# Attention's PSUM banks as two tiles of three and two single ones, with one exponential per three heads

## The chip, the cores and the metric

The kernel runs on one core of a Trainium2 chip, in fp32. The metric is the device time of one execution in microseconds (us). Engines are called as the profile calls them: PE (TensorE, matmuls; PEld are its weight loads), DVE (VectorE), ACT (ScalarE), POOL (GpSimd), SP (SyncE, which issues DMAs here).

## What is computed

One token matrix `x` of 2048 rows and 448 columns goes through an attention with 16 query heads and one shared key and value head (width 28), and through a token- and channel-mixing MLP. A gate mixes the two results:

```
g = sigmoid((x * gate_w).sum(-1))
q = (x @ wq) as 16 heads of 28;  k = x @ wk;  v = x @ wv
p = softmax(q k^T * 28**-0.5);   a = (p v, heads side by side) @ wo
b = x1 + gelu(layernorm(x1) @ w3) @ w4     where x1 = x + shifted gelu(layernorm(x) @ w1) @ w2
out = g * a + (1 - g) * b
```

The change lies in the attention, which fills the second part of the program, from about 400 us on. The MLP before it is left as it was.

## The kernel before

Scores are held with keys on the partitions. A **unit** `u` is one block of 512 queries with one group of four heads; there are 16 units. A unit runs over 16 key tiles `kt` of 128 keys, in 8 **stretches** `v` of two key tiles each. The loop at L1004 counts stretches through all units with `k` (0 to 126; the last stretch is written out behind the loop). All engines' orders are those in which the code is written: the kernel has a manual schedule, so each engine runs its instructions in the order of the Python calls.

In a stretch the following happens, in this order of the calls:

- `scores(u, kt)` (L937 to L943), for the first and then the second key tile. Four heads are computed side by side, each on 32 rows of PE, into four PSUM banks of 512 columns. Each product is split in three passes (`i` = 0, 1, 2 at L939), and the four heads of one pass come one after the other. So all four banks of a key tile are complete with its last pass.
- `exps` (L959). Heads 0, 1 and 2 go through an exponential on ACT from PSUM to SBUF, one instruction per head (L969), as softmax without division. Head 3 is copied by DVE to a tile `pd` (L966). The order in which the banks are read is `READ = (0, 3, 1, 2)`.
- `late_exps` (L974): one exponential on ACT, in place in SBUF, over head 3 of both key tiles (128x1024).
- The **job**: four matmuls of the output product of an earlier unit (`wo_half`, L865, with the matmuls at L843), 32 rows of tokens each, into one bank. DVE adds the result to the output tile (L837). In stretches 2 to 11 the job is a rest of the MLP (`w4_half`, L879). Stretch 0 has three larger ones instead (`w4_job`, L869), stretch 1 has none, and the last unit has two jobs in its last four stretches.
- `values` (L986): probabilities times values for the stretch before this one (`k - 1`), in two halves of 256 query columns. Each half is 16 matmuls into one bank (L979), for four heads side by side, and DVE adds the half to the tile `o` of the unit (L983; a copy at L994 in a unit's first stretch). DVE adds the first half when it is done, and the second in the next stretch's beginning.

The eight banks are in a queue `banks`. `take()` pops the oldest. A bank goes to the end of the queue when its reader has been issued. So a job takes the bank of the first key tile's first head (its exponential is the first to be issued), the first half of the values that of head 3, and the second half that of head 1. A wait is set from who used the bank last: the tiles are tracked one by one.

```
bs = [take() for j in range(4)]                      # L938
for j in READ: ... banks.append(bs[j])               # L961, L970
ps = take(); wo_part(...); evict(...); banks.append(ps)   # job
pv = take(); value(...) x2; add_value(...)           # a half of the values
```

Of the kernel before, what the change touches and what calls it, by code (L numbers as in the profile page):

```python
# [9 lines left out]
F32 = mybir.dt.float32  # L10
F32R = mybir.dt.float32r
AF = mybir.ActivationFunctionType
# [4 lines left out]
P = 128  # L17
S = 2048
D = 448
# [11 lines left out]
SHIFTS = (-1, 1, -2, 2)  # L31
PB = 18
PD = 3
# [9 lines left out]
def gated_mix_kernel(  # L43
# [15 lines left out]
    dram = ctx.enter_context(tc.tile_pool(name="dram", bufs=1, space=bass.MemoryType.DRAM))  # L59
    psA = ctx.enter_context(tc.tile_pool(name="psA", bufs=1, space=PSUM))  # L60
    ctx.enter_context(tc.manual_schedule(
# [136 lines left out]
    def max_tile(name):  # L198
        return psA.tile([P, 512], F32, tag="mx", bufs=1, name=name)
# [566 lines left out]
    ctx2.close()  # L766


    with tc.tile_pool(name="s3", bufs=1, reuse_waits="tile") as s3, \
# [3 lines left out]

        banks = [mm_tile("bank_0"), mm_tile("bank_1"), misc_tile("bank_2"), max_tile("bank_7")]
        banks += [ps3.tile([P, 512], F32, name=f"bank_{i}") for i in range(3, 7)]
# [70 lines left out]
        def wo_end(u, t, ps, evict=by_one, queue=nc.sync, cols=slice(0, D)):  # L846
            b, g = divmod(u, NG)
            n = 4 * b + t
            before = x1[:, n, cols] if g == 0 else ot_of[n][:, cols]
            evict(n, ps, before, cols)  # L850
            banks.append(ps)
# [5 lines left out]
        def wo_job(u, t, cols=slice(0, D), evict=by_one, queue=nc.sync):  # L857
            b, g = divmod(u, NG)
            ps = take()
# [3 lines left out]
            return wo_end(u, t, ps, evict, queue, cols)  # L863

        def wo_half(u, i):  # L865
            t, h = divmod(i, 2)
            wo_job(u, t, slice(224 * h, 224 * h + 224))

        def w4_job(t):  # L869
            n = NT - 4 + t  # L870
            tok = slice(t * P, (t + 1) * P)
            gh, gl = last_g
            ps = bank(f"job_{n}")[:, 0:D]
            nc.tensor.matmul(ps, gh[:, tok], w4h[-1][:, 1, :], start=True, stop=False)
            nc.tensor.matmul(ps, gh[:, tok], w4l[-1][:, 1, :], start=False, stop=False)
            nc.tensor.matmul(ps, gl[:, tok], w4h[-1][:, 1, :], start=False, stop=True)
            nc.vector.tensor_add(x1[:, n, :], x1[:, n, :], ps)

        def w4_half(k, i):  # L879
            t, h = divmod(i, 2)  # L880
            n = NT - 4 + t
            cols = slice(224 * h, 224 * h + 224)
            ps = take()
# [5 lines left out]
            banks.append(ps)  # L889

# [46 lines left out]
        def scores(u, kt):  # L937
            bs = [take() for j in range(4)]  # L938
            for i in range(3):  # L939
                for j in range(4):  # L940
                    for _, _, w, a in score(u, bs[j], j, slice(kt * P, (kt + 1) * P), i=i):
                        nc.tensor.matmul(bs[j], w, a, start=(i == 0), stop=(i == 2), tile_position=(32 * j, 0))  # L942
            return bs  # L943

        p_free = [s3.tile([P, 512], F32, name=f"p_{i}") for i in range(PB)]
        pd_free = [s3.tile([P, 2, 512], F32, name=f"pd_{i}") for i in range(PD)]
# [11 lines left out]

        def exps(u, kt, bs):  # L959
            ps = p_of[u, kt] = {}  # L960
            for j in READ:  # L961
                if j == DRAIN:
                    if kt % 2 == 0:
                        pd_of[u, kt // 2] = turn_of(pd_free)
                    ps[j] = pd_of[u, kt // 2][:, kt % 2, :]
                    nc.vector.tensor_copy(ps[j], bs[j])  # L966
                else:
                    ps[j] = turn_of(p_free)
                    behind[kt % 2] = nc.scalar.activation(ps[j], bs[j], AF.Exp, scale=SCALE)  # L969
                banks.append(bs[j])  # L970

# [10 lines left out]
        def add_value(u, q, pv):  # L982
            nc.vector.tensor_add(o_of[u][:, q], o_of[u][:, q], pv[:, q])  # L983
            banks.append(pv)

        def values(u, v):  # L986
            if v == 0:
                o_of[u] = s3.tile([P, 512], F32, tag="o", bufs=2, name=f"o_{u}")
            for q in HALVES:
                pv = take()  # L990
                for kt in (2 * v, 2 * v + 1):
                    value(u, kt, q, pv, kt % 2 == 0, kt % 2 == 1)
                if v == 0:
                    nc.vector.tensor_copy(o_of[u][:, q], pv[:, q])  # L994
                    banks.append(pv)
                else:
                    add_value(u, q, pv)

        HALVES = (slice(0, 256), slice(256, 512))

        READ = (0, 3, 1, 2)
        DRAIN = 3

        for k in range(NU * NV - 1):  # L1004
            u, v = divmod(k, NV)
            if k == 3:
                q_begin(1)
                q_fetch(2)
            if v == 6 and u + 2 < NU:
                q_begin(u + 2)  # L1010
                q_fetch(u + 3)
            for kt in (2 * v, 2 * v + 1):
                exps(u, kt, scores(u, kt))
            late_exps(u, v)
            if k == 0:
                for t in range(3):
                    w4_job(t)
            if k in (2, 3):
                w4_half(1, k + 4)
            if 4 <= k < 12:  # L1020
                w4_half(0, k - 4)
            if k == 11:
                weigh_x1(NT - 4, NT)
            if v >= 4 and u:
                wo_half(u - 1, v - 4)
            if v < 4 and u > 1:
                wo_half(u - 2, v + 4)
# [34 lines left out]

        blocks = [slice(4 * t, 4 * t + 4) for t in range(4)]
        b14, b15 = [scores(u, kt) for kt in (NT - 2, NT - 1)]
        p14 = p_of[u, NT - 2] = {j: turn_of(p_free) for j in range(DRAIN)}
        p14[DRAIN] = turn_of(pd_free)[:, 0, :]
# [3 lines left out]
        for q in HALVES:  # L1070
            for p, ps in [(p14[1], b14[1]), (p14[2], b14[2]), (p14[DRAIN], p14[DRAIN])] + [(p15[j], b15[j]) for j in READ]:
                nc.scalar.activation(p[:, q], ps[:, q], AF.Exp, scale=SCALE)
# [9 lines left out]
        banks.extend((b14[1], b14[2]))  # L1082
        add_value(u, q0, pvs[0])
        value(u, NT - 3, q1, pvs[1], False, False)
        value(u, NT - 2, q1, pvs[1], False, False)
# [9 lines left out]
        banks.extend(b15)  # L1095
        add_value(u, q1, pvs[1])
        tail_back(blocks[1])
        store0 = wo_job(u, 0, evict=by_two, queue=None)
# [4 lines left out]
        for n in blocks[2:4]:  # L1103
            tail_back(n)
        wo_end(u, 1, joint[1])
        nc.sync.dma_start(*store0)
        joint[3] = take()
# [9 lines left out]
        nc.scalar.activation(redo, tw, AF.Copy, scale=-1.0, bias=float(P))  # L1117
        wo_end(u, 3, joint[3], by_one, nc.scalar)
        again = nc.values_load(redo, min_val=0, max_val=P,
                               skip_runtime_bounds_check_because="it is P less a sum of P zeros and ones")  # L1120
# [60 lines left out]
```

## Time and profile before

| what | us |
|---|---|
| median of 3 runs (lowest, highest) | 911.42 (911.41, 911.49) |
| span of the profiled execution, first to last instruction | 909.8 |
| PE, ACT, DVE busy in the span | 904.0, 634.5, 543.7 |
| first stretch begins (scores of the first key tile) | 400.2 |
| the loop's last stretch ends | 895.4 |

The time of a run is 1.6 us longer than the span of the profiled execution; the trace has no other time for that execution than its span. A matmul's end in the profile is modelled, and four matmuls of a group run side by side. So "busy" for PE says little, and the starts of groups say more: they are given in rows of the timeline, with start and duration in us, engine, line, operation, `out<-in`, the shape, the count `x`, and in square brackets the idle time before with what ended it.

### The profile page before, as it was taken

To read this page: it belongs to the slowest core of one execution; us is meant where nothing else is said; L and a number is where in the kernel's file an instruction comes from. 1 tells how busy PE (TensorE), PEld (TensorE's weight loads), DVE (VectorE), ACT (ScalarE), POOL (GpSimd) and SP (SyncE) were. 2 spreads that over 40 slices of the span, in tenths; PEclk is the share of its full clock that TensorE was granted. 3 is DMA by queue.
4 is the path that set the end of the run, shared out by engine and by line. 5 is a ranking of instruction groups with operands and counts; after the bars stand their busy time and mean duration, and the time that the engine had idled before them with its cause. 6 is when DMAs were issued, how large, how long until landed. Compare 5 with 4: busy or idle time off the path is not lost.

```text
span 909.8 us, 24136 instructions
## 1 busy us (share of the span) xinstructions
PE 904.0 (99%) x10101; PEld 643.8 (71%) x10101; DVE 543.7 (60%) x1083; ACT 634.5 (70%) x1139; POOL 108.0 (12%) x140
## 2 busy tenths in 40 slices
PE   9999999999999999999999999999999999999998
PEld 7788888888888888875566656556666556666654
DVE  4665264631435736546666666676666667666675
ACT  5542255432131222159999999999999999999996
POOL 3143200212000440002200000000000000000000
PEclk9999999999999999999999999999999999999999
DMA  9822543220222042120000001100011000010001
GB/s 304 296 76 42 162 145 125 39 68 21 39 61 61 16 108 63 29 65 23 26 25 4 26 14 50 30 26 26 3 46 46 26 3 26 14 56 13 15 14 44
DMA packets 41808, 51.81 MB, mean 57 GB/s; under 512 B 9312, under 2 KB 27552, under 8 KB 41696
## 3 DMA queue, kind: packets, MB, share of 16 engines
q1 hardware_dynamic: 38528, 44.54, 17.2%
q10 hardware_dynamic: 3168, 5.70, 1.8%
q8 instruction: 80, 1.31, 0.6%
q14 instruction: 32, 0.26, 0.1%
HBM read 37.04 MB, written 11.93 MB: 54 GB/s over the span
## 4 chain that ended last, share of the span: by engine, by line
PE 99%; ACT 0%; DVE 0%; issue 0%; ACTq 0%; DVEq 0%
PE bank L979 24%; PE bank L942 22%; PE bank L843 8%; PE acc L693 5%; PE acc L692 5%; PE acc L694 5%; PE g L132 4%; PE g L131 4%; PE g L133 4%; PE hs L460 1%; PE hs L461 1%; PE g L135 1%; PE g L134 1%; PE h L131 1%; PE h L132 1%; PE h L133 1%
## 5 line engine op out<-in xcount | busy, mean ns | idle before, releaser
L969 ACT ACTIVATE p<-bank 128x512 f32<-128x512 f32 x762 | 386.9, 615 | 1.6 <-PE bank L942 1.5
L979 PE MATMUL bank<-p,vext 128*32 128x256 f32 x3076 | 244.4, 379 | 0.0
L979 PE MATMUL bank<-pd,vext 128*32 128x256 f32 x1020 | 241.1, 379 | 0.0
L966 DVE COPY pd<-bank 128x512 f32<-128x512 f32 x254 | 175.3, 691 | 51.1 <-PE bank L942 49.6
L979 PEld LDWEIGHTS bank<-p,vext 128*32 128x32 f32 x3076 | 126.4, 110 | 82.2 <-ACT p L969 0.5
L681 ACT ACTIVATE gh<-g 128x512 fp32r<-128x512 f32 x54 | 32.3, 599 | 180.6 <-PE g L135 180.6
L983 DVE TENSOR_TENSOR o<-o,bank 128x256 f32<-128x256 f32 x222 | 93.6, 421 | 91.9 <-ACT p L969 53.9
L974 ACT ACTIVATE pd<-pd 128x1024 f32<-128x1024 f32 x127 | 140.4, 1106 | 0.0
L942 PE MATMUL bank<-qh,kH 30*128 30x512 f32 x1024 | 117.3, 443 | 0.0
L979 PEld LDWEIGHTS bank<-pd,vext 128*32 128x32 f32 x1020 | 111.8, 110 | 0.1
L684 DVE TENSOR_TENSOR gl<-gf,gh 128x512 fp32r<-128x512 f32 x54 | 37.2, 689 | 116.6 <-ACT gf L682 116.5
L942 PE MATMUL bank<-qh,kL 28*128 28x512 f32 x1024 | 104.8, 392 | 0.0
L942 PE MATMUL bank<-ql,kH 28*128 28x512 f32 x1024 | 104.6, 391 | 0.0
L942 PEld LDWEIGHTS bank<-qh,kH 30*128 30x128 f32 x1024 | 60.7, 182 | 56.5 <-ACT p L969 46.0
L693 PE MATMUL acc<-w4l,gh 128*128 128x448 f32 x216 | 78.9, 365 | 0.0
L692 PE MATMUL acc<-w4h,gh 128*128 128x448 f32 x216 | 78.8, 365 | 0.0
L694 PE MATMUL acc<-w4h,gl 128*128 128x448 f32 x216 | 78.7, 364 | 0.0
L843 PE MATMUL bank<-wof,on 128*32 128x224 f32 x1008 | 73.1, 367 | 0.0
L132 PE MATMUL g<-al,w3h 128*128 128x512 f32 x168 | 65.8, 392 | 0.0
L131 PE MATMUL g<-ah,w3h 128*128 128x512 f32 x168 | 65.6, 390 | 0.0
L133 PE MATMUL g<-ah,w3l 128*128 128x512 f32 x168 | 65.5, 390 | 0.0
L942 PEld LDWEIGHTS bank<-ql,kH 28*128 28x128 f32 x1024 | 51.8, 185 | 8.5
(205 smaller groups left out, 1168.7 us busy)
## 6 DMA issues: line engine op xcount, KB each, us to landing
qd<-qf ACTq DMA_DIRECT2D x16, 256.0 KB
qm<-qd SPq DMA_DIRECT2D x16, 256.0 KB
qr<-qd SPq DMA_DIRECT2D x16, 256.0 KB
rb<-rd SPq DMA_DIRECT2D x15, 256.0 KB
x<-in_x_dram SPq DMA_DIRECT2D x4, 896.0 KB
xd<-xt SPq DMA_DIRECT2D x16, 224.0 KB
w34raw<-in_w_dram SPq DMA_DIRECT2D x7, 512.0 KB
w34raw<-in_w_dram SPq DMA_DIRECT2D x7, 448.0 KB
```

The source lines that it names most:

```text
L131: nc.tensor.matmul(ps, wh[:, c, :], ah[:, c, :], start=(c == 0), stop=False)
L132: nc.tensor.matmul(ps, wh[:, c, :], al[:, c, :], start=False, stop=False)
L133: nc.tensor.matmul(ps, wl[:, c, :], ah[:, c, :], start=False, stop=False)
L692: nc.tensor.matmul(ps, gh[:, tok], w4h[i][:, k, :], start=(f == 0), stop=False)
L693: nc.tensor.matmul(ps, gh[:, tok], w4l[i][:, k, :], start=False, stop=False)
L694: nc.tensor.matmul(ps, gl[:, tok], w4h[i][:, k, :], start=False, stop=(f == stop))
L843: nc.tensor.matmul(ps[32 * j:32 * j + 32, cols], on_of[u][:, tok], wof[:, u % NG, cols], start=start, stop=stop, tile_position=(0, 32 * j))
L942: nc.tensor.matmul(bs[j], w, a, start=(i == 0), stop=(i == 2), tile_position=(32 * j, 0))
L966: nc.vector.tensor_copy(ps[j], bs[j])
L969: behind[kt % 2] = nc.scalar.activation(ps[j], bs[j], AF.Exp, scale=SCALE)
L974: ins = nc.scalar.activation(pd, pd, AF.Exp, scale=SCALE)
L979: nc.tensor.matmul(pv[32 * j:32 * j + 32, q], vext[:, kt, :], p_of[u, kt][j][:, q], start=start, stop=stop, tile_position=(0, 32 * j))
```

## The change

The queue of eight banks is replaced by fixed places. `wide[0]` and `wide[1]` are PSUM tiles of three banks, `single[0]` and `single[1]` are of one. Key tile `kt` puts heads 0 to 2 into `wide[kt % 2]` and head 3 into `single[kt % 2]`.

One ACTIVATE of 128x1536 takes the three heads of a key tile, in place of three of 128x512. The probabilities go to tiles of three heads (`PG = 6` tiles where there were `PB = 18` single ones: the same room). DVE's copy of head 3 is issued ahead of the exponential.

The halves of the values go into `single[0]` and `single[1]`, and the job goes into bank 0 of `wide[0]` (a second one into bank 1), between the two halves. `values` is now called twice, once for each half.

The pool of the four older banks is closed ahead of the attention, so that all eight can be laid out anew. The code behind the loop is the same but for the bookkeeping of the banks.

```diff
-        def exps(u, kt, bs):
-            ps = p_of[u, kt] = {}
-            for j in READ:
-                if j == DRAIN:
-                    if kt % 2 == 0:
-                        pd_of[u, kt // 2] = turn_of(pd_free)
-                    ps[j] = pd_of[u, kt // 2][:, kt % 2, :]
-                    nc.vector.tensor_copy(ps[j], bs[j])
-                else:
-                    ps[j] = turn_of(p_free)
-                    behind[kt % 2] = nc.scalar.activation(ps[j], bs[j], AF.Exp, scale=SCALE)
-                banks.append(bs[j])
+        def exps(u, kt):
+            if kt % 2 == 0:
+                pd_of[u, kt // 2] = turn_of(pd_free)
+            pd = pd_of[u, kt // 2][:, kt % 2, :]
+            nc.vector.tensor_copy(pd, single[kt % 2])
+            pg = turn_of(pg_free)
+            behind[kt % 2] = nc.scalar.activation(pg, wide[kt % 2], AF.Exp, scale=SCALE)
+            p_of[u, kt] = [pg[:, j, :] for j in range(3)] + [pd]
...
-            bs = [take() for j in range(4)]
+            bs = [wide[kt % 2][:, j, :] for j in range(3)] + [single[kt % 2]]
...
+        def values(u, v, i):
...
+            q, pv = HALVES[i], single[i]
+            for kt in (2 * v, 2 * v + 1):
+                value(u, kt, q, pv, kt % 2 == 0, kt % 2 == 1)
...
             for kt in (2 * v, 2 * v + 1):
-                exps(u, kt, scores(u, kt))
+                scores(u, kt)
+                exps(u, kt)
             late_exps(u, v)
+            job = wide[0][:, 0, :]
             if k == 0:
-                for t in range(3):
-                    w4_job(t)
+                for t, ps in enumerate((*single, job)):
+                    w4_job(t, ps)
+            if k:
+                values(*divmod(k - 1, NV), 0)
...
             if v >= 4 and u:
-                wo_half(u - 1, v - 4)
+                wo_half(u - 1, v - 4, job)
...
             if v >= 4 and u == NU - 1:
-                wo_half(u - 1, v)
+                wo_half(u - 1, v, wide[0][:, 1, :])
             if k:
-                values(*divmod(k - 1, NV))
+                values(*divmod(k - 1, NV), 1)
```

The order of PE at one ordinary stretch before: the last score matmul of the second key tile, the job (`wof`), the two halves of the values (`vext`), and the next stretch's first score. `bank_3` held the first key tile's head 0, `bank_1` its head 3, `bank_6` its head 1. The name in brackets is the engine whose semaphore is waited for.

```order
L942 MATMUL bank_4_3497<-ql_10_7604,kH_1030 128x512
L843 MATMUL bank_3_3496<-wof_3490,on_8_7958 32x224 [waits Activation_49]
L843 MATMUL bank_3_3496<-wof_3490,on_8_7958 32x224 x3
L979 MATMUL bank_1_3493<-p_0_3506,vext_73 32x256 [waits DVE_49]
...
L979 MATMUL bank_6_3499<-p_0_3506,vext_73 32x256 [waits Activation_49]
...
L942 MATMUL bank_5_3498<-qh_10_7603,kH_1030 128x512 [waits Activation_49]
```

The same place after. `single_0` held the first key tile's head 3, `wide_0` its heads 0 to 2, `single_1` the second key tile's head 3.

```order
L948 MATMUL single_1_3496<-ql_13_8618,kH_1030 128x512
L982 MATMUL single_0_3494<-p_0_3503,vext_73 32x256 [waits DVE_49]
...
L982 MATMUL single_0_3494<-pd_0_3509,vext_73 32x256 [waits Activation_49]
L847 MATMUL wide_0_3493<-wof_3491,on_11_8945 32x224 [waits Activation_49]
L847 MATMUL wide_0_3493<-wof_3491,on_11_8945 32x224 x3
L982 MATMUL single_1_3496<-p_0_3503,vext_73 32x256 [waits DVE_49]
...
L948 MATMUL wide_0_3493<-qh_13_8617,kH_1030 128x512 [waits DVE_49]
```

Directly behind the scores stood the job, which waits for ACT. Now the first half of the values stands there, which waits for DVE's copy out of `single_0`, and the job comes behind it. The next stretch's scores now wait for DVE, which must have taken the job out of `wide_0`.

ACT in one stretch before: six exponentials from banks and the late one.

```order
L969 ACTIVATE p_6_3512<-bank_2_3494 128x512 [waits PE_49]
L969 ACTIVATE p_7_3513<-bank_3_3496 128x512 [waits PE_49]
L969 ACTIVATE p_8_3514<-bank_1_3493 128x512 [waits PE_49]
L969 ACTIVATE p_9_3515<-bank_5_3498 128x512 [waits PE_49]
L969 ACTIVATE p_10_3516<-bank_0_3492 128x512 [waits DVE_49,PE_49]
L969 ACTIVATE p_11_3517<-bank_4_3497 128x512 [waits DVE_49,PE_49]
L974 ACTIVATE pd_1_3525<-pd_1_3525 128x1024 [waits DVE_49,Activation_49]
```

And after, a whole stretch:

```order
L972 ACTIVATE p_0_3503<-wide_0_3493 128x1536 [waits DVE_49,PE_49]
L972 ACTIVATE p_1_3504<-wide_1_3495 128x1536 [waits PE_49]
L977 ACTIVATE pd_0_3509<-pd_0_3509 128x1024 [waits DVE_49,Activation_49]
```

Seven instructions became three; each wide one waits for the last pass of all its three heads.

More of the change, by code (lines that the diff above doesn't have):

```diff
@@ L31 @@
 SHIFTS = (-1, 1, -2, 2)
-PB = 18
+PG = 6
 PD = 3
@@ L59, in gated_mix_kernel @@
     dram = ctx.enter_context(tc.tile_pool(name="dram", bufs=1, space=bass.MemoryType.DRAM))
-    psA = ctx.enter_context(tc.tile_pool(name="psA", bufs=1, space=PSUM))
+    psA_stack = ExitStack()
+    psA = psA_stack.enter_context(tc.tile_pool(name="psA", bufs=1, space=PSUM, reuse_waits="tile"))
     ctx.enter_context(tc.manual_schedule(
@@ L772, in gated_mix_kernel @@
         nc.sync.dma_start(wof, wo.rearrange("(g p) n -> p g n", p=P))
-        banks = [mm_tile("bank_0"), mm_tile("bank_1"), misc_tile("bank_2"), max_tile("bank_7")]
-        banks += [ps3.tile([P, 512], F32, name=f"bank_{i}") for i in range(3, 7)]
+        wide, single = [], []
+        for i in range(2):
+            wide.append(ps3.tile([P, 3, 512], F32, name=f"wide_{i}"))
+            single.append(ps3.tile([P, 512], F32, name=f"single_{i}"))
+        banks = []
         def take():
@@ L855, in wo_end, with wo_job @@
             return store
-        def wo_job(u, t, cols=slice(0, D), evict=by_one, queue=nc.sync):
+        def wo_job(u, t, cols=slice(0, D), evict=by_one, queue=nc.sync, ps=None):
             b, g = divmod(u, NG)
-            ps = take()
+            own = ps is None
+            if own:
+                ps = take()
             wo_part(u, t, cols, ps, True, True)
@@ L862, in wo_job, with wo_half, w4_job @@
                 ot_of[4 * b + t] = s3.tile([P, D], F32, tag="ot", bufs=5, name=f"ot_{4 * b + t}")
-            return wo_end(u, t, ps, evict, queue, cols)
-        def wo_half(u, i):
+            store = wo_end(u, t, ps, evict, queue, cols)
+            if own:
+                banks.append(ps)
+            return store
+        def wo_half(u, i, ps):
             t, h = divmod(i, 2)
-            wo_job(u, t, slice(224 * h, 224 * h + 224))
-        def w4_job(t):
+            wo_job(u, t, slice(224 * h, 224 * h + 224), ps=ps)
+        def w4_job(t, ps):
             n = NT - 4 + t
@@ L872, in w4_job @@
             gh, gl = last_g
-            ps = bank(f"job_{n}")[:, 0:D]
+            ps = ps[:, 0:D]
             nc.tensor.matmul(ps, gh[:, tok], w4h[-1][:, 1, :], start=True, stop=False)
@@ L943, in scores @@
             return bs
-        p_free = [s3.tile([P, 512], F32, name=f"p_{i}") for i in range(PB)]
+        pg_free = [s3.tile([P, 3, 512], F32, name=f"p_{i}") for i in range(PG)]
+        p_free = [pg[:, j, :] for pg in pg_free for j in range(3)]
         pd_free = [s3.tile([P, 2, 512], F32, name=f"pd_{i}") for i in range(PD)]
@@ L983, in add_value @@
             nc.vector.tensor_add(o_of[u][:, q], o_of[u][:, q], pv[:, q])
-            banks.append(pv)
-        def values(u, v):
-            if v == 0:
[L988 to L997, printed above, removed]
+        def values(u, v, i):
+            if v == 0 and i == 0:
+                o_of[u] = s3.tile([P, 512], F32, tag="o", bufs=2, name=f"o_{u}")
+            q, pv = HALVES[i], single[i]
+            for kt in (2 * v, 2 * v + 1):
+                value(u, kt, q, pv, kt % 2 == 0, kt % 2 == 1)
+            if v == 0:
+                nc.vector.tensor_copy(o_of[u][:, q], pv[:, q])
+            else:
+                add_value(u, q, pv)
         HALVES = (slice(0, 256), slice(256, 512))
-        READ = (0, 3, 1, 2)
         DRAIN = 3
@@ L1024, in gated_mix_kernel @@
             if v >= 4 and u:
-                wo_half(u - 1, v - 4)
+                wo_half(u - 1, v - 4, job)
             if v < 4 and u > 1:
-                wo_half(u - 2, v + 4)
+                wo_half(u - 2, v + 4, job)
             if v >= 4 and u == NU - 1:
-                wo_half(u - 1, v)
+                wo_half(u - 1, v, wide[0][:, 1, :])
             if k:
-                values(*divmod(k - 1, NV))
+                values(*divmod(k - 1, NV), 1)
             if u and v == 0:
@@ L1064, in gated_mix_kernel @@
         b14, b15 = [scores(u, kt) for kt in (NT - 2, NT - 1)]
+        p_free = [pg[:, j, :] for pg in pg_free for j in range(3)]
         p14 = p_of[u, NT - 2] = {j: turn_of(p_free) for j in range(DRAIN)}
@@ L1070, in gated_mix_kernel @@
         for q in HALVES:
-            for p, ps in [(p14[1], b14[1]), (p14[2], b14[2]), (p14[DRAIN], p14[DRAIN])] + [(p15[j], b15[j]) for j in READ]:
+            for p, ps in [(p14[1], b14[1]), (p14[2], b14[2]), (p14[DRAIN], p14[DRAIN])] + [(p15[j], b15[j]) for j in (0, 3, 1, 2)]:
                 nc.scalar.activation(p[:, q], ps[:, q], AF.Exp, scale=SCALE)
@@ L1083, in gated_mix_kernel @@
         add_value(u, q0, pvs[0])
+        banks.append(pvs[0])
         value(u, NT - 3, q1, pvs[1], False, False)
@@ L1096, in gated_mix_kernel @@
         add_value(u, q1, pvs[1])
+        banks.append(pvs[1])
         tail_back(blocks[1])
@@ L1105, in gated_mix_kernel @@
         wo_end(u, 1, joint[1])
+        banks.append(joint[1])
         nc.sync.dma_start(*store0)
@@ L1118, in gated_mix_kernel @@
         wo_end(u, 3, joint[3], by_one, nc.scalar)
+        banks.append(joint[3])
         again = nc.values_load(redo, min_val=0, max_val=P,
```

10 lines of the change are left out of this document (4 added, 6 removed).

## The prediction

> **What bounds the kernel now.** First the page: the span, the busy time, ACT's forty slices, and the chain that ended last.
>
> ```profile
> span 909.8 us, 24136 instructions
> PE 904.0 (99%) x10101; PEld 643.8 (71%) x10101; DVE 543.7 (60%) x1083; ACT 634.5 (70%) x1139; POOL 108.0 (12%) x140
> ACT  5542255432131222159999999999999999999996
> PE 99%; ACT 0%; DVE 0%; issue 0%; ACTq 0%; DVEq 0%
> ```
>
> The chain lies on PE alone, but ACT is full from the 18th slice on, which is where the attention begins. The table by stretches of time says the same for the attention's middle:
>
> ```profile
> 410.00:880.00 470.00, 470.00 (x7740) 282.92 (x7732) 322.34 (x649) 469.94 (x847) 32.48 (x32) 1.00 0.09 24
> ```
>
> PE 470.00 and ACT 469.94 of 470.00: two engines look full, and the granted clock is 1.00. To see which one waits, I take one stretch of the timeline, engine by engine. ACT:
>
> ```profile
> 606.00 0.64 ACT L969 ACTIVATE p<-bank 128x512 f32<-128x512 f32 x1
> 606.48 1.11 ACT L974 ACTIVATE pd<-pd 128x1024 f32<-128x1024 f32 x1
> 607.49 3.04 ACT L969 ACTIVATE p<-bank 128x512 f32<-128x512 f32 x6
> 610.37 1.10 ACT L974 ACTIVATE pd<-pd 128x1024 f32<-128x1024 f32 x1
> ```
>
> Six exponentials start within 610.37 - 607.49 = 2.88 us, 0.48 each, and the late one occupies 607.49 - 606.48 = 1.01. Their sum, 3.89, is the stretch: ACT never pauses. PE, with the weight loads that waited:
>
> ```profile
> 606.49 0.51 PE L942 MATMUL bank<-qh,kH 30*128 30x512 f32 x4
> 607.06 0.42 PE L942 MATMUL bank<-ql,kH 28*128 28x512 f32 x4
> 607.29 0.42 PE L942 MATMUL bank<-qh,kH 30*128 30x512 f32 x4
> 607.76 0.41 PE L942 MATMUL bank<-ql,kH 28*128 28x512 f32 x4
> 608.13 0.16 PEld L843 LDWEIGHTS bank<-wof,on 128*32 128x32 f32 x8 [0.39 <-ACT p L969]
> 608.14 0.58 PE L843 MATMUL bank<-wof,on 128*32 128x224 f32 x8
> 608.54 0.39 PE L979 MATMUL bank<-p,vext 128*32 128x256 f32 x3
> 610.05 0.39 PE L979 MATMUL bank<-p,vext 128*32 128x256 f32 x3
> 610.38 0.51 PE L942 MATMUL bank<-qh,kH 30*128 30x512 f32 x4
> ```
>
> From scores to scores 610.38 - 606.49 = 3.89 too. Groups of score matmuls come every 0.23, but from the last one (607.76) to the job (608.14) pass 0.38: the job waits for ACT's first exponential of this stretch. From the last group of the values (610.05) to the next scores (610.38) pass 0.33. The waits below put such a gap down to ACT too, but no exponential ends there: ahead of the scores at 606.49 the last one ran until 606.64 and the one before it, 0.48 earlier, until 606.16. So I take the 0.33 for the turn from one shape of matmul to the other. Then only some 0.05 (0.38 less 0.33) of PE's 3.89 is waiting. Both engines are bounds within 0.05 us of each other.
>
> ```profile
> PEld bank L843 <- ACT p L969: 46.2, 114, 0.4
> PEld bank L942 <- ACT p L969: 44.9, 109, 0.4
> PEld bank L979 <- DVE pd L966: 0.4, 1, 0.4
> ```
>
> Of these rows of the waits (406 to 890 us) the first and the last matter most for what follows: the job waits for ACT in nearly every stretch, and the values waited for DVE's copy of head 3 once in the whole attention. DVE in the same stretch shows why:
>
> ```profile
> 606.69 0.42 DVE L983 TENSOR_TENSOR o<-o,bank 128x256 f32<-128x256 f32 x1 [0.50 <-ACT p L969]
> 607.59 1.40 DVE L966 COPY pd<-bank 128x512 f32<-128x512 f32 x2 [0.48 <-PE bank L942]
> 608.90 0.44 DVE L837 SCALAR_TENSOR_TENSOR ot<-bank,gg,ot 128x224 f32<-128x224 f32 x1
> 901.21 0.31 DVE L1061 STREAM_TRANSPOSE on<-scaled 128x128 f32<-128x128 f32 x1
> 901.58 0.16 PEld L843 LDWEIGHTS bank<-wof,on 128*32 128x32 f32 x8 [0.49 <-DVE on L1061]
> L966 DVE COPY pd<-bank 128x512 f32<-128x512 f32 x254 | 175.3, 691 | 51.1 <-PE bank L942 49.6
> ```
>
> DVE sits idle until the scores are done, and starts the first copy 0.11 after the last pass ends (607.06 + 0.42 = 607.48, then 607.59). One copy takes 0.69. From DVE's end to PE's start pass 901.58 - 901.52 = 0.06 (the pair of rows from the tail). So the bank of head 3 is free for PE at 607.59 + 0.69 + 0.06 = 608.34. The values come at 608.54: the job, standing between, hides that wait with 0.20 to spare.
>
> **The change, part by part.** Times are now counted from the first score matmul of a stretch (606.49 is 0).
>
> *What moves.* The first half of the values now stands directly behind the scores, and writes into `single[0]`, which DVE has to empty. PE meets that wait uncovered. The copy starts at 1.10, ends at 1.79, and PE goes on at 1.85. Before, PE went on at 1.65 (608.14), with the job. What follows is the same number of matmuls in the same shapes, only with the job between the halves: before from 1.65 to 3.89, that is 2.24. After: half (4 groups of the 8 that start between 608.54 and 610.05, seven pitches in 1.51, so 0.216 a group, 0.86), job 0.40 (608.54 - 608.14), half and turn 0.65 + 0.33: also 2.24. The stretch becomes 1.85 + 2.24 = 4.09, longer by 0.20. Queued behind the waiting matmul on PE are the job, the other half and the next scores, and for the next scores wait ACT and, through its copy, DVE: the loop scores, copy, half, job, half, scores closes on itself, so a delay is not made up.
>
> *What is removed.* ACT issues three instructions for seven. The trace has no exponential of 1536 columns; the nearest rows are these:
>
> ```profile
> L969 ACT ACTIVATE p<-bank 128x512 f32<-128x512 f32 x762 | 386.9, 615 | 1.6 <-PE bank L942 1.5
> L618 ACT CAST ah<-xr 128x512 fp32r<-128x512 f32 x16 | 8.8, 618 | 11.4 <-DMA xr<-xd 11.4
> L106 ACT CAST w1h<-w1raw 128x1344 fp32r<-128x1344 f32 x1 | 1.3, 1317 | 0.5 <-DVE st_s L139 0.5
> ```
>
> The two casts give (1317 - 618) / 832 = 0.84 ns a column, so 1536 columns take 615 + 1024 x 0.84 = 1475 ns. The overlap between two exponentials is 0.615 - 0.48 = 0.135, so one occupies ACT for 1.34. Bounds: 1.45 for three pitches of 0.48, and 1.85 for three whole ones of 0.615; I take 1.475, since columns are what grows in both rows. ACT then needs 2 x 1.34 + 1.01 = 3.69 a stretch, 0.20 less than before. In a stretch of 4.09 that leaves ACT idle for 0.40: its gain is worth nothing where PE waits for DVE.
>
> The Trainium skill, "ScalarE: Activation LUTs", section "What ACT_TABLE_LOAD costs", gives an ACTIVATE 186 ns plus 0.833 ns a column, of which some 93 ns overlap with the next one. The trace agrees on 512 columns (613 against 615), not on the pitch (520 against 480). By the page four instructions fewer save an estimated 0.37 a stretch on ACT; the sum stays as it is, as it doesn't run through ACT.
>
> *New waits, with their cover.* The job waits for the wide exponential of the first key tile. From PE's end to ACT's start:
>
> ```profile
> 895.95 0.41 PE L942 MATMUL bank<-ql,kH 28*128 28x512 f32 x4
> 896.38 0.60 ACT L1069 ACTIVATE p<-bank 128x512 f32<-128x512 f32 x1 [0.29 <-PE bank L942]
> ```
>
> 0.02 (896.36 to 896.38). The last pass ends at 0.99, so the exponential runs from 1.01 to 2.48, and PE could go on at 2.53. The job's turn comes at 1.85 + 0.86 = 2.71: covered by the copy's wait and the half, with 0.18 to spare. At the upper bound (1.85) it would come at 2.91 and cost 0.20 more.
>
> The next scores wait until DVE has taken out the job: job from 2.71, its matmuls done at 3.29 (0.58), 0.11 to DVE, 0.44 there, 0.06 back: 3.90, against 4.09. Covered by the second half, 0.19 to spare. The second half waits for the second copy: 1.79 + 0.69 + 0.06 = 2.54, against 3.11. The second key tile's head 3 waits for the addition of the second half: 606.69 is 0.20, and 0.42 + 0.06 later is 0.68, against 0.80 (607.29). The wide exponential of the second key tile ends far ahead of its next use. The late exponential is done 0.7 into the next stretch, ahead of 1.85. All nothing, each with 0.1 us or more.
>
> *The first stretch* has three MLP jobs in place of one small one:
>
> ```profile
> 401.44 1.30 DVE L966 COPY pd<-bank 128x512 f32<-128x512 f32 x2
> 401.88 0.47 PE L874 MATMUL bank<-w4h,gh_late 128*128 128x448 f32 x1
> 402.86 1.16 DVE L877 TENSOR_TENSOR x<-x,bank 128x448 f32<-128x448 f32 x2
> 403.60 0.36 PE L876 MATMUL bank<-w4h,gl_late 128*128 128x448 f32 x1
> 403.89 0.51 PE L942 MATMUL bank<-qh,kH 30*128 30x512 f32 x4
> ```
>
> The first job now waits for the first copy: 401.44 + 0.69 + 0.06 = 402.19, where it came at 401.88. The nine matmuls' last start lies 403.60 - 401.88 = 1.72 later, at 403.91, and ends at 404.27. The next scores need the bank of that last job: 0.11, an addition of 0.58 (half of 1.16), 0.06: 405.02, where they came at 403.89. That is 1.1, once.
>
> *The rest.* Stretch 1 has no job and I count it at nothing. The code behind the loop issues the same instructions. DMAs and POOL's work keep their places; the room in SBUF is the same.
>
> **Sum.** Stretches 2 to 126 are 125: 125 x 0.20 = 25.0, and 1.1: 26.1. Against the profiled execution that is 909.8 + 26.1 = 935.9, and 1.6 us lie around its span (median of the runs 911.42): 937.5. The error of the rows is 0.01 to 0.02 each, some 0.04 on the 0.20, hence 5 us on the sum, and the small covers of 0.1 to 0.2 could each leak a few hundredths: 927 to 947.
>
> **Rivals.**
>
> *ACT sets the pace, faster.* For it speaks that ACT is full, and that a stretch is the sum of its instructions. If the time followed ACT, a stretch fell to 3.69 and the kernel by 125 x 0.20 = 25 us, to 886. Against it speaks PE: the values cannot come closer to the scores than the turn of 0.33, at 1.27 + 0.33 = 1.60 (607.76 is 1.27), so with no wait at all a stretch takes 3.84, and the time is 911.4 - 125 x 0.05 + 1.1 = 906. It decides from the point at which the copy's wait ends before 1.65, so the copy must be done 0.20 sooner than the rows say. The Trainium skill, "ScalarE: Activation LUTs", in the same section, is this rival's rule: fewer, longer ACTIVATEs pay the fixed part less often. Chance 0.07, for 886 to 908.
>
> *No change.* Were the copy's start, its 0.69 or PE's restart together shorter by 0.20 but not by more, the stretch would stay. Chance 0.03, 910 to 913.
>
> *The wide exponential is slow.* If it takes as long as three single ones (1.85), the job waits for it on top, 0.20 more: 937.5 + 25 = 962. Reading three banks in one instruction is shown by no row. Chance 0.06, 948 to 962.
>
> **How the numbers follow.** My forecast has the rest, 0.84, with 927 to 947 and its middle at 937.5. The range 927 to 948 takes in that case and the lower edge of the slow exponential, and leaves out the faster rival, no change and most of the slow one, together with what may be off in the forecast's own edges: 2 in 10. Some 0.2% (1.8 us) is what a measurement of this kernel can tell from no change. Faster 0.07, same 0.03, slower 0.90 (forecast and slow exponential).
>
> **What would show it.** In the profile after: a stretch of 4.09 from scores to scores; the weight load of the values' first half waiting for DVE `pd` in nearly every stretch, and the job's wait for ACT gone; the first half starting 1.85 after the scores; the wide exponential at 1.47 with ACT idle for 0.4 a stretch until PE's scores; 1.1 us more up to the second stretch. Wrong I would be if the values' first half started at 1.6 (the copy sooner than I read), if ACT stayed full, if the job still waited for ACT, or if the scores began waiting for DVE's work on the job.

## The result and the profile after

| | before | after |
|---|---|---|
| median of 4 runs each (lowest, highest), us | 911.45 (911.41, 912.12) | 940.07 (939.35, 940.79) |
| span of the profiled execution, us | 909.8 | 939.0 |
| ratio of the times, 95% interval | | 1.0313 (1.0298 to 1.0328) |

The changed kernel is 3.1% slower. 937.5 was forecast, and 940.07 lies in the range of 927 to 948. The page of after, its span, busy times, ACT's forty slices, the chain by engine, and two of the groups:

```profile
span 939.0 us, 23471 instructions
PE 910.6 (97%) x10101; PEld 640.3 (68%) x10101; DVE 554.5 (59%) x1083; ACT 614.9 (65%) x631; POOL 107.6 (11%) x140
ACT  5542354322222222189999999999999999999983
PE 86%; DVE 12%; issue 1%; ACT 1%; DVEq 0%
L972 ACT ACTIVATE p<-wide 128x1536 f32<-128x1536 f32 x254 | 354.7, 1449 | 40.7 <-PE single L948 24.6
L970 DVE COPY pd<-single 128x512 f32<-128x512 f32 x254 | 175.5, 691 | 53.1 <-PE single L948 31.6
```

DVE, which had 0% of the chain of before, now holds 12% of it. ACT lost 508 instructions and 20 us of busy time, and it now idles 40.7 us ahead of the wide exponentials, until PE's scores. The slices still print a 9 nearly everywhere, so they can't show this; the table by stretches of time does (columns: length, PE, PEld, DVE, ACT, POOL busy, granted clock, DMA share, GB/s):

```profile
440.00:900.00 460.00, 445.82 (x7288) 263.15 (x7284) 315.51 (x614) 425.59 (x342) 27.55 (x28) 1.00 0.09 24
```

ACT 425.59 of 460: 0.30 us idle in each stretch of 4.04, where before had none. PE too is no longer full. What it waits for stands in the waits (406 to 900 us: total us, times, longest):

```profile
PEld single L982 <- DVE pd L970: 68.1, 122, 0.6
PEld wide L948 <- DVE ot L841: 40.1, 97, 0.6
```

The values waited for DVE's copy of head 3 once before, and 122 times now; the job's wait for ACT (114 times before) is gone. The second row looks like a new wait for the job's addition. One stretch of the timeline tells whether it is one:

```profile
612.37 0.50 PE L948 MATMUL wide<-qh,kH 30*128 30x512 f32 x3
613.39 2.79 ACT L972 ACTIVATE p<-wide 128x1536 f32<-128x1536 f32 x2 [0.30 <-PE single L948]
615.77 0.45 DVE L841 SCALAR_TENSOR_TENSOR ot<-wide,gg,ot 128x224 f32<-128x224 f32 x1
616.07 1.06 ACT L977 ACTIVATE pd<-pd 128x1024 f32<-128x1024 f32 x1
616.10 0.39 PE L982 MATMUL single<-p,vext 128*32 128x256 f32 x3
616.43 0.50 PE L948 MATMUL wide<-qh,kH 30*128 30x512 f32 x3
617.00 0.39 PE L948 MATMUL wide<-ql,kH 28*128 28x512 f32 x2
617.44 2.79 ACT L972 ACTIVATE p<-wide 128x1536 f32<-128x1536 f32 x2 [0.31 <-PE wide L948]
617.48 1.40 DVE L970 COPY pd<-single 128x512 f32<-128x512 f32 x2 [0.49 <-PE wide L948]
618.22 0.42 PE L982 MATMUL single<-p,vext 128*32 128x256 f32 x3
619.11 0.56 PE L847 MATMUL wide<-wof,on 128*32 128x224 f32 x8
```

The addition ends at 616.22 (615.77 + 0.45) and the scores start at 616.43. They don't wait for it: the profile names the last semaphore in a gap that is the turn of the shapes, 0.33 from the last group of the values (616.10) as before. The copy's wait is real: the first copy ends at 618.17 (617.48 + 0.69), and the first half starts 0.05 later, at 618.22. That is 1.79 after the scores, where PE went on at 1.65 before. Nothing else stands between.

Of the 29.2 us that the span grew by, the traces give each part, by the starts of the score blocks (the 24 score matmuls that open each stretch):

| part | before | after | more, us |
|---|---|---|---|
| up to the first scores | 400.19 | 401.10 | 0.9 |
| first stretch | 3.70 | 5.50 | 1.8 |
| stretches 1 and 2 | 7.95 | 7.71 | -0.2 |
| stretches 3 to 123, mean of 121 | 3.890 | 4.043 | 18.5 |
| stretches 124 to 126, the ones with two jobs, mean | 4.27 | 5.27 | 3.0 |
| last stretch and what follows, to the end | 14.4 | 19.6 | 5.2 |

The 0.9 arises in the first 12 us, while the first inputs are loaded, by lines that the change doesn't touch; it isn't the change's. In the traces of the five kernels below, all built on the changed one, the first scores start between 399.80 and 400.78. In the first stretch ACT, PE and DVE of after show two steps:

```profile
402.16 1.28 ACT L972 ACT_TABLE_LOAD   x1 [2.29 <-issue]
403.45 2.79 ACT L972 ACTIVATE p<-wide 128x1536 f32<-128x1536 f32 x2
404.96 0.19 PEld L882 LDWEIGHTS wide<-w4h,gh_late 128*128 128x128 f32 x1 [0.75 <-ACT p L972]
406.60 0.19 PEld L948 LDWEIGHTS wide<-qh,kH 30*128 30x128 f32 x3 [1.14 <-DVE x L885]
```

ACT loads its table for the exponential only when the first key tile's scores are there, at 402.16, and so the wide exponential starts at 403.45 and the third MLP job waits for it until 404.96. What held the load back the profile doesn't name (`issue`). In before the same load began ahead of the scores and was over at 400.25, and ACT then stood idle for 0.94 until the first scores were there:

```profile
398.97 1.28 ACT L969 ACT_TABLE_LOAD   x1
401.19 2.07 ACT L969 ACTIVATE p<-bank 128x512 f32<-128x512 f32 x4 [0.94 <-PE bank L942]
```

The stretches with two jobs, of after:

```profile
906.27 0.56 PE L847 MATMUL wide<-wof,on 128*32 128x224 f32 x8
906.97 0.45 DVE L841 SCALAR_TENSOR_TENSOR ot<-wide,gg,ot 128x224 f32<-128x224 f32 x1
907.47 0.16 PEld L847 LDWEIGHTS wide<-wof,on 128*32 128x32 f32 x8 [1.07 <-DVE ot L841]
```

The second job goes into another bank, but of the same tile `wide[0]` whose first bank DVE is still reading, and waits until DVE is done (907.42). Without a wait it would come 0.40 after the first, at 906.67: 0.8 a stretch. And the end, behind the last scores:

```profile
919.39 0.50 PE L948 MATMUL wide<-qh,kH 30*128 30x512 f32 x3
922.26 1.25 ACT L1076 ACTIVATE p<-wide 128x256 f32<-128x256 f32 x4
923.56 0.42 PE L982 MATMUL wide<-p,vext 128*32 128x256 f32 x3 [2.49 <-ACT p L1076]
927.02 0.66 PE L982 MATMUL single<-p,vext 128*32 128x256 f32 x3
927.45 0.66 PE L982 MATMUL single<-p,vext 128*32 128x256 f32 x3
930.79 0.54 PEld L847 LDWEIGHTS wide<-wof,on 128*32 128x32 f32 x16 [1.56 <-ACT y L837]
```

The values come 4.17 after the scores (923.56 - 919.39), where it was 1.65 before, because they need a bank of a tile that the exponentials are still reading: 2.5 of the 5.2. Then they run at half the pace (groups 0.43 apart, 927.02 to 927.45), and the output products wait for a reader of their tile (last row).

### The profile page after: what moved, and what is told of

It reads as the page before. It is cut to its first block, busy times and chain, and to the rows that moved or that the text cites. A ratio compares the mean times of both kernels' runs of the same rounds, so it can differ in the third digit from the quotient of the medians.

```text
span 939.0 us, 23471 instructions
## 1 busy us (share of the span) xinstructions
PE 910.6 (97%) x10101; PEld 640.3 (68%) x10101; DVE 554.5 (59%) x1083; ACT 614.9 (65%) x631; POOL 107.6 (11%) x140
## 4 chain that ended last, share of the span: by engine, by line
PE 86%; DVE 12%; issue 1%; ACT 1%; DVEq 0%
PE single L982 26%; PE wide L948 11%; DVE pd L970 9%; PE wide L847 5%; PE acc L694 5%; PE acc L693 5%; PE acc L695 5%; PE g L133 4%; PE g L132 4%; PE g L134 4%; PE hs L461 1%; PE hs L462 1%; PE g L136 1%; PE g L135 1%; PE h L132 1%
## 5 line engine op out<-in xcount | busy, mean ns | idle before, releaser
L972 ACT ACTIVATE p<-wide 128x1536 f32<-128x1536 f32 x254 | 354.7, 1449 | 40.7 <-PE single L948 24.6
L982 PE MATMUL single<-p,vext 128*32 128x256 f32 x3050 | 268.1, 383 | 15.6
L982 PE MATMUL single<-pd,vext 128*32 128x256 f32 x1014 | 264.1, 383 | 0.0
L970 DVE COPY pd<-single 128x512 f32<-128x512 f32 x254 | 175.5, 691 | 53.1 <-PE single L948 31.6
L982 PEld LDWEIGHTS single<-p,vext 128*32 128x32 f32 x3050 | 113.4, 110 | 129.8 <-DVE pd L970 70.4
L977 ACT ACTIVATE pd<-pd 128x1024 f32<-128x1024 f32 x127 | 134.6, 1060 | 0.0
L948 PE MATMUL wide<-qh,kH 30*128 30x512 f32 x768 | 116.0, 444 | 0.9 <-DVE x L885 0.8
L948 PE MATMUL single<-qh,kH 30*128 30x512 f32 x256 | 113.3, 442 | 0.0
L948 PE MATMUL wide<-ql,kH 28*128 28x512 f32 x768 | 103.0, 391 | 0.0
L948 PE MATMUL wide<-qh,kL 28*128 28x512 f32 x768 | 102.9, 391 | 0.0
L982 PEld LDWEIGHTS single<-pd,vext 128*32 128x32 f32 x1014 | 101.4, 110 | 0.0
```

Source lines behind the costliest of these rows:

```text
L970: nc.vector.tensor_copy(pd, single[kt % 2])
L972: behind[kt % 2] = nc.scalar.activation(pg, wide[kt % 2], AF.Exp, scale=SCALE)
L977: ins = nc.scalar.activation(pd, pd, AF.Exp, scale=SCALE)
L982: nc.tensor.matmul(pv[32 * j:32 * j + 32, q], vext[:, kt, :], p_of[u, kt][j][:, q], start=start, stop=stop, tile_position=(0, 32 * j))
```

## The experiments

The theory: what a stretch lasts is set by where PE can go on behind the scores, and in after that is DVE's copy of head 3. The rival: the wide exponential, or three banks in one tile, sets it. A second question is where the 10 us come from that the steady stretches don't explain. All are compared with the kernel before on the same chip (911.93, median of 15 runs; for the fourth 911.78, of 7).

**Half the copy.** DVE copies 256 of head 3's 512 columns; half of head 3's probabilities are left out. POOL sets the tiles `pd` to zero once, ahead of the loop (this part of the edit is not shown).

```diff
-            nc.vector.tensor_copy(pd, single[kt % 2])
+            nc.vector.tensor_copy(pd[:, 0:256], single[kt % 2][:, 0:256])
```

> The changed kernel, but DVE copies only 256 of head 3's 512 columns out of the single bank (the other half of head 3's probabilities is left out of the computation and stays near a constant). Theory, the uncovered wait for the copy sets the stretch: the copy takes about 0.42 us in place of 0.69, so the first half of the values could start at 1.53 after the scores, and then starts at 1.60, as close as the turn from scores allows. The job would then come at 2.48 and meets the wide exponential's end (2.52): a stretch of 3.88 in place of 4.04, 121 x 0.16 = 19.5 us less, about 920.5 us. Rival, the wait stands where ACT or PE would wait anyway: no change, 940 us.

Measured: 922.47 (4 runs), ratio 1.0117 (1.0101 to 1.0132); the ordinary stretch 3.90. Timeline, and below it the waits (406 to 890 us):

```profile
611.73 0.50 PE L948 MATMUL wide<-qh,kH 30*128 30x512 f32 x3
612.75 2.79 ACT L974 ACTIVATE p<-wide 128x1536 f32<-128x1536 f32 x2 [0.16 <-PE single L948]
612.78 0.42 DVE L972 COPY pd<-single 128x256 f32<-128x256 f32 x1 [0.49 <-PE single L948]
613.34 0.42 PE L984 MATMUL single<-p,vext 128*32 128x256 f32 x3
614.25 0.16 PEld L847 LDWEIGHTS wide<-wof,on 128*32 128x32 f32 x8 [0.32 <-ACT p L974]
```

```profile
PEld single L984 <- DVE pd L972: 45.4, 124, 0.4
PEld wide L847 <- ACT p L974: 36.7, 113, 0.3
```

The copy is 0.27 shorter, and the first half starts at 1.61 (613.34 - 611.73) for 1.79; this is the turn of the shapes after the last score group, and the 0.4 of the first row is that turn. The stretch is 0.14 shorter: the copy set it. A new limit appears at once. The wide exponential ends at 614.20 (1.45 behind 612.75), and the job waits for it until 614.25. So a shorter copy alone brings this order of the work to 3.90 and no further, and that is no better than the 3.89 of before.

**The job first.** The values' first half goes back behind the job, with the tiles of after.

```diff
-            if k:
-                values(*divmod(k - 1, NV), 0)
             if k in (2, 3):
...
             if k:
+                values(*divmod(k - 1, NV), 0)
+            if k:
                 values(*divmod(k - 1, NV), 1)
```

> The changed kernel, but with the job ahead of both halves of the values, where it stood before. Theory, the job has to wait for the wide exponential of the first key tile, which ends at 2.47 after the scores where the old exponential of one head ended at 1.60: job at 2.52, stretch 2.52 + 2.24 = 4.76, 121 x 0.72 = 87 us more than the changed kernel, about 1027 us; the wait for DVE's copy vanishes. Rival, the fixed places cost the same in any order: about 940 us.

Measured: 1030.72 (1 run, so without an interval; its trace gives the stretch, 4.766). Timeline:

```profile
609.83 0.50 PE L948 MATMUL wide<-qh,kH 30*128 30x512 f32 x3
610.84 2.79 ACT L972 ACTIVATE p<-wide 128x1536 f32<-128x1536 f32 x2 [1.03 <-PE single L948]
612.35 0.16 PEld L847 LDWEIGHTS wide<-wof,on 128*32 128x32 f32 x8 [1.28 <-ACT p L972]
614.59 0.50 PE L948 MATMUL wide<-qh,kH 30*128 30x512 f32 x3
```

The job takes a bank that is free only when all three heads are through, at 2.52, and 2.24 later come the next scores. So the move of the values belongs to the wide tile: it replaces a wait of 2.52 by one of 1.79. What the two parts cost together against before can't be pulled apart into two prices that add. The expected 1027 left out stretches 2 and 124 to 126, which grew by 0.72 like the others: 2.9 us.

**Three exponentials.** The tiles and the order of after, with three instructions of 512 columns for the wide one.

```diff
-            behind[kt % 2] = nc.scalar.activation(pg, wide[kt % 2], AF.Exp, scale=SCALE)
+            for j in range(3):
+                behind[kt % 2] = nc.scalar.activation(pg[:, j, :], wide[kt % 2][:, j, :], AF.Exp, scale=SCALE)
```

> The changed kernel's places and order, but three exponentials of 512 columns in place of a wide one. Theory, ACT's gain is worth nothing here: ACT needs 3.88 a stretch, less than the 4.04 that PE's loop through the copy takes, and the third exponential ends at 2.58, ahead of the job's turn (2.67): 940 us, within 2 us. Rival, the wide exponential's saving keeps the loss small, so without it each stretch grows by the 0.20 it saves: 964 us.

Measured: 940.24 (4 runs), ratio 1.0305 (1.0290 to 1.0321), the stretch 4.044. The table by stretches of time:

```profile
440.00:880.00 440.00, 426.39 (x6972) 242.89 (x6972) 301.53 (x587) 433.67 (x763) 27.55 (x28) 1.00 0.09 25
```

ACT is busy for 433.67 of 440, and the kernel takes as long as after does. The gain of the wide exponential on ACT is worth nothing in this order; the rival falls.

**The one-off parts.** Behind the loop the scores and values get eight single banks in a pool of their own; in the stretches with two jobs both are computed ahead of DVE's two additions; an exponential of four columns loads ACT's table early. Cut to its core:

```diff
+        nc.scalar.activation(s3.tile([P, 4], F32, name="table"), powt, AF.Exp)
...
+            if v >= 4 and u == NU - 1:
+                two = [(v - 4, wide[0][:, 0, :]), (v, wide[0][:, 1, :])]
+                for i, ps in two: wo_part(...)
+                for i, ps in two: wo_end(...)
...
+        tail_banks = [ps4.tile([P, 512], F32, name=f"tail_{i}") for i in range(8)]
```

> The changed kernel with three edits outside of the ordinary stretch. The code behind the loop gets eight single banks in place of two tiles of three and two single ones; the two jobs of the last unit's stretches are both computed before DVE takes the first one out; an exponential of four columns, ahead of the attention, loads ACT's table early. Theory, a PSUM tile is waited for as a whole, so the wide tiles cost 5.2 us behind the loop (the values waited for exponentials of other heads in the same tile, the output products for each other's evictions) and 0.85 us in each of the last three stretches, and the table's 1.28 us lie open once for about 0.65: 940.1 - 5.2 - 2.6 - 0.65 = 931.7 us, with ordinary stretches unchanged at 4.04. Rival, the end is longer because PE's clock fell to 0.66 there for another reason than waiting: it falls here too, and no more than 3.5 us go.

Measured: 932.73 (4 runs), ratio 1.0225 (1.0208 to 1.0242); span 930.7. By the score blocks the ordinary stretch stays at 4.042, the first one falls from 5.50 to 4.84, the three with two jobs from 5.27 to 4.66, and the end from 19.6 to 14.3, which is before's 14.4. Timeline:

```profile
399.56 1.28 ACT L773 ACT_TABLE_LOAD   x1
401.86 2.79 ACT L974 ACTIVATE p<-wide 128x1536 f32<-128x1536 f32 x2 [0.80 <-POOL ones L958]
907.04 0.19 PEld L950 LDWEIGHTS wide<-qh,kH 30*128 30x128 f32 x3 [0.62 <-DVE ot L843]
918.00 0.12 PEld L984 LDWEIGHTS tail<-p,vext 128*32 128x32 f32 x3 [0.38 <-ACT p L1082]
```

The table is loaded by 400.84, 1.02 ahead of the first exponential, and the last values come 1.62 after theirs (918.00 - 916.38). All three parts are shown, and with them 0.66 + 3 x 0.6 + 5.3 = 7.8 us. The two jobs gave 0.6 a stretch for an expected 0.85, since the next scores now wait for DVE's second addition (third row).

**One bank more for the first head.** The places are fixed, as in after, but head 0 has a tile of one bank (`lone`), heads 1 and 2 one of two, head 3 a single one; the order of the work is that of before, with the job in `lone[0]` right behind the scores. The eight banks behind the loop and the early table are as in the last experiment; the second job of the last unit's stretches goes into a bank of `wide[0]`, between the halves of the values. ACT issues two exponentials per key tile. Cut to its core:

```diff
+            lone.append(ps3.tile([P, 512], F32, name=f"lone_{i}"))
-            wide.append(ps3.tile([P, 3, 512], F32, name=f"wide_{i}"))
+            wide.append(ps3.tile([P, 2, 512], F32, name=f"wide_{i}"))
...
-            behind[kt % 2] = nc.scalar.activation(pg, wide[kt % 2], AF.Exp, scale=SCALE)
+            nc.scalar.activation(pg[:, 0, :], lone[kt % 2], AF.Exp, scale=SCALE)
+            behind[kt % 2] = nc.scalar.activation(pg[:, 1:3, :], wide[kt % 2], AF.Exp, scale=SCALE)
```

> The order of before (scores, scores, job, half, half) with fixed places: head 0 in a bank of its own, heads 1 and 2 in a tile of two banks with one exponential of 1024 columns, head 3 in a bank of its own; the job goes into head 0's bank, the halves into head 3's banks. The tail has eight single banks, and the table of the exponential is loaded early. ACT needs about 3.78 a stretch in place of 3.88. Theory, before was held by PE's loop scores, exponential of head 0, job, values as much as by ACT: stretch 1.63 + 2.24 = 3.87, 910 us, at most 2 us below before. Rival, ACT alone held it: a stretch falls with ACT's sum to 3.78 or PE's floor of 3.84, 899 to 906 us.

Measured: 911.08 (11 runs), ratio 0.9989 (0.9980 to 0.9998); the stretch is 3.883 for 3.887 (medians). Timeline, and the table by stretches of time:

```profile
606.34 1.08 ACT L981 ACTIVATE pd<-pd 128x1024 f32<-128x1024 f32 x1
606.46 0.18 PEld L951 LDWEIGHTS lone<-qh,kH 30*128 30x128 f32 x1 [0.41 <-DVE o L990]
607.45 0.60 ACT L975 ACTIVATE p<-lone 128x512 f32<-128x512 f32 x1
608.10 0.16 PEld L850 LDWEIGHTS lone<-wof,on 128*32 128x32 f32 x8 [0.40 <-ACT p L975]
610.34 0.18 PEld L951 LDWEIGHTS lone<-qh,kH 30*128 30x128 f32 x1 [0.41 <-DVE o L990]
```

```profile
440.00:880.00 440.00, 440.00 (x7250) 263.73 (x7242) 304.00 (x609) 436.98 (x568) 26.29 (x27) 1.00 0.09 25
```

PE goes on at 1.64, as soon as the first head is through, and 2.24 later (610.34) come the next scores: the stretch of before, with two instructions fewer on ACT, and ACT no longer full (436.98 of 440). The idle time understates ACT's room: the first exponential starts 1.11 after the late one (607.45 - 606.34), and in before, where nothing made it wait, 1.01. So ACT has 0.10 a stretch to spare and the stretch did not shorten. The time differs from before's by a tenth of a per cent, with an interval that just excludes none; that is the same time for any practical purpose. The hoped-for 899 to 906 of an ACT that set the pace did not come.

## Why the prediction was right, and where its sum was off

- **Where the stretch closes** was right. PE waits in nearly every stretch for DVE's copy, uncovered, with the job's wait gone. Four kernels follow one rule: stretch = time at which PE goes on behind the scores + 2.24. 1.65 gives 3.89 (before, from which the 2.24 was read), 1.79 gives 4.03 (after: 4.04), 2.52 gives 4.76 (job first: 4.77), 1.64 gives 3.88 (one bank more for the first head: 3.88). Half the copy doesn't follow it: PE goes on at 1.61, but meets a second wait behind that, the job's until 2.52, and the stretch is counted from there: 2.52 + 0.40 + 0.65 + 0.33 = 3.90. The 2.24 was right within 0.01.
- **The 0.20 a stretch** was over-sized: 0.153. The first half started at 1.79, not at 1.85. The copy itself took its 0.69, but began at 1.05 instead of 1.10; PE followed the copy by 0.05, not by 0.06. In the stretches shown the last pass of the first key tile ends 0.96 after the first one began (0.99 before, by a row of all four heads). In the median of 100 stretches of each trace it ends at 0.97 in both, so it is DVE that follows sooner, after 0.08 instead of 0.12; why is not known. These few hundredths make 5.7 us over 121 stretches, a little more than the error of 5 that the prediction allowed for.
- **The wide exponential** took 1449 ns for a forecast 1475, and the late one 1060 (1106 before). Two wide ones take 2.68 (613.39 to 616.07), 1.34 each, as worked out. ACT idles 0.30 a stretch and not 0.40, because the stretch is 0.05 shorter, and because the late exponential occupies 1.06 for 1.01: with idle time behind it, nothing overlaps its end. One instruction that reads three banks takes what its columns give: the slow exponential (1.85) did not happen.
- **The covers** held. The job's wait for the exponential (2.53 against 2.71) never showed in after; it showed when the copy was halved, at the 2.52 forecast for it. The next scores did not wait for the job's addition, though the waits name it: in the ordinary stretches it ended 0.1 us or more ahead of them, 0.2 in the median, with one exception (0.055).
- **The first stretch**, 1.1 forecast, cost 1.8. The working looked at PE and DVE, and not at what ACT's first exponential has in front of it: a table load of 1.28, which in before was hidden, as it was over 0.94 ahead of the first exponential, and in after began only behind the first scores. Moved away, it gave 0.66, as expected: 1.1 is what is left.
- **"The code behind the loop issues the same instructions"** was the step that failed. It does, and nothing was counted for it; it cost 5.2. The tail writes values into banks that the exponentials of the last key tile were just done with, and a tile of three banks is waited for as a whole. In eight single banks the 5.2 are gone. Some 1.1 of the 5.2 came of the slower clock that followed the pause there: half the copy has the same code behind its loop and the same pause, but kept its clock, and its end takes 18.5 against 19.6.
- **The last unit's second jobs** were counted like all others at 0.2 each; they cost 1.0. Same reason: the first job's bank and the second's are one tile. It was shown by computing both before DVE's additions, which gave back 0.6 of the 0.8.
- So the sum came out 2.2 us short (26.1 against 29.2 - 0.9 = 28.3) by two errors of opposite sign. That 937.5 came so near to 940.07 is luck in that part: the errors are 6 and 8 us. Stretches 1 to 123: 24.4 forecast, 18.3 measured. The parts that run once: 1.1 + 3 x 0.2 = 1.7 forecast, 1.8 + 3.0 + 5.2 = 10.0 measured.
- **The rival in which ACT sets the pace** falls by the fifth kernel. With PE going on at 1.64 again and ACT having 0.10 a stretch to spare, the time stays, as PE's loop of scores, first exponential, job, values and turn needs 3.88 by itself.
- Two slips in the working changed nothing: ACT's slices are full from the 19th on, not the 18th (which prints 5, as the attention begins within it), and three pitches of 0.48 are 1.44, not 1.45.

What stays open: whether a version with one exponential for three heads can come under the 3.89 of before, towards 3.84, the stretch without any wait. It would need the first two products behind the scores to go to banks that neither ACT nor DVE reads at that time, and I see no such place among eight banks. That is argued, and wasn't tried.

## What to carry to other kernels

In a loop that closes through one engine, cost each order by the moment at which that engine can go on, and let everything behind it be a constant, unless a second wait shows up there (as with half the copy); an instruction saved on another "full" engine is worth only what that moment moves by. Making buffers larger moves that moment to the last reader of the whole buffer, so price it in every place that uses a part of it: the prologue and the epilogue too, where no steady state hides anything. A table or a set-up that an engine loads in front of its first instruction must be looked for when that instruction is changed: here ACT stood idle for 2.29 us in front of the load.

## What the runs showed of the hardware

The granted clock fell behind the loop in after, and not in the kernel whose code there has eight single banks. The table by stretches of time, of after and then of that kernel (length, PE, PEld, DVE, ACT, POOL, clock):

```profile
919.40:923.50 4.10, 1.67 (x28) 1.12 (x24) 1.11 (x2) 3.09 (x11) 0.00 (x0) 1.00 0.00 0
925.00:928.00 3.00, 3.00 (x36) 1.53 (x32) 0.98 (x3) 0.00 (x0) 0.00 (x0) 0.50 0.00 0
```

```profile
920.00:922.00 2.00, 2.00 (x38) 1.25 (x36) 1.21 (x4) 1.86 (x7) 0.10 (x1) 1.00 0.00 0
```

PE stood for 2.49 us (until 923.56), ran at full speed for 1.3, and then at 0.50 for 3.4 us (924.85 to 928.25): groups of the values came 0.43 apart for 0.216. Seven such pitches (924.89 to 927.88) cost PE 1.5 us. The Trainium skill, "TensorE: Matmul & The Clock Gate", section "What's actually happening", gives an idle window of about 3.4 us, free-running, after which the clock is halved. The length of the slow part agrees with that; the pause here was shorter than such a window.

Such a pause need not bring the slow clock. Three of the experiments have the same code behind the loop. In the job first and in three exponentials PE stands for 2.49 too, and the clock is at 0.50 as soon as it goes on (1013.20 to 1014.70, and 923.00 to 924.50). In half the copy PE stands for 2.50, and the clock stays at 1.00 (904.50 to 912.00). The times of after spread in the same way: with a mean clock of 1.0 it took 939.35 and 939.54, with 0.998 and 0.997 it took 940.79 and 940.60. Where the clock fell is shown for the profiled execution alone (940.79). Pauses of 0.85 in every stretch (the job first) left the clock at 1.00 from 440 to 880.

The gap of 0.33 from the last values to the next scores stands in after as in before (616.10 to 616.43), and the profile names another end of it each time: ACT before, DVE's `ot` after, DVE's `o` in the fifth kernel. The Trainium skill, "TensorEngine Tiling (Array Packing)", section "Key Properties", says that a change of the tiling mode drains TensorE; the scores use 30 rows, the values 32 columns, and the rows agree with it in that the gap is 0.11 more than the pitch of a group (0.33 less 0.216). That the 0.11 is such a drain is not shown.
